# A new load order, fewer fillers, a shorter softmax and fewer copies at the start of a convolution and SwiGLU kernel

## The chip, the cores and the metric

The kernel runs on one core of one Trainium2 chip. The metric is the device time of one execution in microseconds (us); lower is better. It is about 1.8 us more than the span that the profile shows.

In this text TensorE is the matmul engine (PE in the profile, PEld for its weight loads), VectorE is DVE, ScalarE is ACT, GpSimd is POOL. L384 is a line of the kernel file. Each variant has its own file, so the same matmul has slightly different line numbers in different kernels.

## The reference, cut to what matters

```python
w = softmax(weight)                    # 8 heads x 7 taps
x_pad = zeros(6 rows) + x              # x: 8 x 4096 x 192, fp32
y = sum over k of w[h, k] * x_pad[s + k, head h]     # causal convolution of 7 taps
g = y @ w_gate                         # 192 -> 1536
out = (g * sigmoid(g) * (y @ w_val)) @ w_out         # 1536 -> 192, 32768 rows
```

## The kernel before

The 32768 rows are worked in 64 blocks of 512. In the steady state, each block takes 12 steps of gate and value matmuls (128 columns of the 1536 each), a SiLU on ScalarE, a product on VectorE, and the down projection, which trails behind. The convolution is itself a matmul with a band matrix made from the taps.

Blocks 0 to 3 have a special path (`early`), because nothing has been convolved when the kernel starts. The start has these parts.

The loads. All of them are issued from GpSimd, and they cast fp32 to fp16 on the way:

```python
    xe_load(0)                                  # x of block 0, three transfers
    for f0, f1 in ((0, 384), (384, 960), (960, Dff)):
        load_w(f0, f1)                          # gate and value weights, three transfers each
    xe_tile(1)
    xe_load(1)                                  # x of block 1, two transfers
    load_wo(0, 6)                               # down weights
    xe_tile(2)
    xe_load(2)
    load_wo(6, NCH)
    xe_tile(3)
    xe_load(3)
    # ... then the large x loads of the later blocks
```

The softmax of the taps, and its split into two fp16 parts:

```python
    seq(nc.vector.tensor_reduce(wmax, wraw, axis=AX.X, op=ALU.max))
    seq(nc.vector.tensor_scalar(wraw, wraw, scalar1=wmax, scalar2=None, op0=ALU.subtract))
    seq(nc.scalar.activation(wexp[:, 0:K], wraw, AF.Exp))
    # ... sum and reciprocal on VectorE
    seq(nc.vector.tensor_scalar(split[:, 0, 0:K], wexp[:, 0:K], scalar1=wsum, scalar2=None, op0=ALU.mult))
    # ... scalar_tensor_tensor writes split[:, 1], the rest
```

TensorE's own chain. Fillers are matmuls on zeros that only keep it busy:

```python
    keep_warm(11)         # 11 fillers, 128 x 512
    spread_taps()         # 16 tiny matmuls: taps to 128 partitions; VectorE then makes `spread`
    keep_warm(3)
    make_wide()           # 4 matmuls 128 x 512, then copies: the band matrix `wide`
    early(0, ...)         # convolution of block 0: 64 matmuls, then copies to `tme`
    eturn(0, ...)         # 15 transposes
    for n in range(n_steps):
        # ... after the gate and value matmuls of step 4: early(1), the convolution of block 1;
        #     step 7: first down projection; step 10: early(2)
```

The copies in `early`, four per block, two of them on each engine:

```python
        for hh in range(2):
            for r, (g0, g1) in enumerate(ER):       # 288 and 192 columns
                # ...
                seq((act, dve)[(hh + r) % 2](tme[e][...], o[...]))
        seq(dve(tme[e][:, :, SL * Q : 4 * Q], tme[e][:, :, 0:Q]))
```

## Time and profile before

| | |
|---|---|
| time, median of 3 runs | 796.1 us (795.15 to 796.2) |
| span of the profiled run | 794.0 us |
| TensorE busy | 784.4 us, 99% |
| TensorE waits for x of block 1 | until 16.44 us |

The first line below is from the profile's page (busy time, share of the span and number of instructions by engine). The second is the page's chain of work that ended last, by engine.

```profile
PE 784.4 (99%) x12023; PEld 494.3 (62%) x12023; DVE 584.7 (74%) x938; ACT 522.3 (66%) x910; POOL 67.4 (8%) x93
PE 97%; POOL 1%; DMA 1%; DVE 0%; ACT 0%; issue 0%; POOLq 0%
```

TensorE is the bound, and nearly all the idle time left is at the start. The next lines are TensorE's timeline there: start in us, duration in us, engine and line, operation, out<-in, count; in brackets the idle time before and what ended it.

```profile
1.20 4.21 PE L648 MATMUL warm<-fill 128*128 128x512 f16 x11 [1.20 <-DVE fill L91]
5.35 0.26 PE L290 MATMUL tapbank<-eye,split 8*32 8x8 f16 x16
5.54 0.82 PE L648 MATMUL warm<-fill 128*128 128x512 f16 x3
6.39 1.02 PE L330 MATMUL taps<-spread,shift 128*128 128x512 f16 x4
7.97 0.83 PE L384 MATMUL cv<-xe,wide 64*64 64x72 f16 x64 [0.56 <-ACT wide L342]
9.74 1.00 PE L443 MATMUL turn<-ident,tme 128*128 128x128 f16 x15 [0.95 <-DVE tme L403]
...
15.24 0.19 PE L384 MATMUL cv<-xe,wide 64*64 64x72 f16 x1 [0.65 <-DMA xe<-in_x_dram]
16.44 0.72 PE L384 MATMUL cv<-xe,wide 64*64 64x48 f16 x63 [1.01 <-DMA xe<-in_x_dram]
```

The first gate matmul is at 10.70 us, in the cut. The last two lines are the convolution of block 1, waiting for its x. The chain of waits in order of time (start, us, what) says why that x comes so late:

```profile
1.41 2.05 POOL xe L97 x3
3.46 4.70 POOL w L162 x8
...
8.88 0.65 POOL xe L97
9.53 6.87 DMA xe<-in_x_dram
```

GpSimd first issues x of block 0 and all nine weight transfers. Then x of block 1 is issued, and it needs almost 7 us behind them.

### The profile page before, as it was taken

The page shows a single profiled execution, that of the slowest core. Times are in us where ns is not written, and L with a number is a line of the kernel's source. Part 1 is how long each engine was busy: PE and PEld are TensorE (multiplying, and loading weights), DVE is VectorE, ACT ScalarE, POOL GpSimd, SP SyncE. Part 2 cuts the span into 40 slices and gives each one's busy share as a digit, 9 for nine tenths or more (in the row PEclk, how much of TensorE's full clock was granted, in tenths as well). Part 3 has the DMA queues.
Part 4 walks back from the last instruction along what each step waited for, and adds up shares of the span by engine and source line. Part 5 has one row for each costly group of instructions (what it writes and reads, how often), then busy time and mean ns, then how long its engine had stood idle before and what let it go on. Part 6 is the DMA issues. An engine that isn't in the chain of part 4 may idle for free.

```text
span 794.0 us, 28606 instructions
## 1 busy us (share of the span) xinstructions
PE 784.4 (99%) x12023; PEld 494.3 (62%) x12023; DVE 584.7 (74%) x938; ACT 522.3 (66%) x910; POOL 67.4 (8%) x93
## 2 busy tenths in 40 slices
PE   7999999999999999999999999999999999999997
PEld 3666666666666666666666666666666666666665
DVE  6777768777777777777777677777777777777775
ACT  5666666666666666766666666666666667666664
POOL 8111001010100101001010010100001010000000
PEclk9999999999999999999999999999999999999999
DMA  9999677785957778477795679857579884725311
GB/s 133 143 193 135 136 122 116 164 130 126 124 108 158 118 157 130 97 143 125 150 130 114 121 116 162 133 124 124 108 157 118 151 118 114 140 79 121 75 42 42
DMA packets 214961, 99.23 MB, mean 125 GB/s; under 512 B 148776, under 2 KB 213936, under 8 KB 213936
## 3 DMA queue, kind: packets, MB, share of 16 engines
q1 hardware_dynamic: 167424, 78.75, 48.7%
q0 software_dynamic: 47136, 18.45, 21.4%
q8 instruction: 94, 1.54, 0.8%
q14 instruction: 35, 0.29, 0.1%
q10 hardware_dynamic: 272, 0.20, 0.1%
HBM read 36.90 MB, written 41.16 MB: 98 GB/s over the span
## 4 chain that ended last, share of the span: by engine, by line
PE 97%; POOL 1%; DMA 1%; DVE 0%; ACT 0%; issue 0%; POOLq 0%
PE gate L550 61%; PE acc L576 32%; PE cv L474 2%; PE val L550 1%; DMA xe<-in_x_dram 1%; POOL w L162 1%; POOL xe L97 0%; PE acc L597 0%; PE cv L384 0%; PE turn L443 0%; DVE h L561 0%; ACT sig L559 0%; DVE o_sb L632 0%; DVE tm L491 0%; ACT o_sb L736 0%
## 5 line engine op out<-in xcount | busy, mean ns | idle before, releaser
L561 DVE TENSOR_TENSOR h<-sig,val 128x512 f16<-128x512 f16 x768 | 507.9, 688 | 196.0 <-PE val L550 190.7
L559 ACT ACTIVATE sig<-gate 128x512 f16<-128x512 f32 x768 | 458.7, 597 | 233.8 <-PE val L550 206.1
L550 PE MATMUL val<-xc,w 64*128 64x512 f16 x2304 | 539.1, 376 | 0.2 <-DVE tm L491 0.2
L550 PE MATMUL gate<-xc,w 64*128 64x512 f16 x2304 | 539.2, 376 | 0.0
L550 PEld LDWEIGHTS <-w 64*128 64x128 f16 x4608 | 221.1, 94 | 212.7 <-issue 1.6
L576 PE MATMUL acc<-wo,h 64*128 64x192 f16 x6096 | 298.9, 243 | 0.0
L576 PEld LDWEIGHTS <-h 64*128 64x128 f16 x6096 | 257.8, 94 | 66.0 <-issue 6.1
L97 POOL DMA_DIRECT2D x<-in_x_dram x40 | 31.6, 791 | 439.3 <-ACT sig L559 429.4
L491 ACT CAST tm<-cv 128x480 f16<-128x480 f32 x60 | 30.6, 562 | 22.1 <-PE cv L474 21.3
L491 DVE CAST tm<-cv 128x480 f16<-128x480 f32 x60 | 36.6, 652 | 2.5
L632 DVE COPY o_sb<-acc 128x384 f32<-128x384 f32 x63 | 34.7, 551 | 0.0
L502 POOL COPY tm<-tm 128x1280 f16<-128x1280 f16 x15 | 18.8, 1254 | 137.4 <-DVE tm L491 122.6
L631 ACT COPY o_sb<-acc 128x384 f32<-128x384 f32 x63 | 30.2, 479 | 0.0
L474 PE MATMUL cv<-x,band 64*32 64x240 f16 x960 | 18.2, 265 | 0.0
L474 PEld LDWEIGHTS <-band 64*32 64x32 f16 x960 | 10.1, 91 | 4.8 <-issue 4.6
L132 POOL MEMSET x<- 6x192 f16 x7 | 1.7, 248 | 59.7 <-PE cv L474 59.6
L648 PE MATMUL warm<-fill 128*128 128x512 f16 x14 | 5.0, 521 | 1.2 <-DVE fill L91 1.2
L403 ACT CAST tme<-cv 128x288 f16<-128x288 f32 (+1 forms) x8 | 2.9, 359 | 5.0 <-PE cv L384 3.6
L97 POOL DMA_DIRECT2D xe<-in_x_dram x9 | 6.0, 679 | 0.3 <-issue 0.3
L384 PE MATMUL cv<-xe,wide 64*64 64x48 f16 (+1 forms) x256 | 3.2, 192 | 2.2 <-DMA xe<-in_x_dram 1.7
L384 PEld LDWEIGHTS <-wide 64*64 64x64 f16 x256 | 2.7, 108 | 3.6 <-DMA xe<-in_x_dram 1.8
L403 DVE CAST tme<-cv 128x192 f16<-128x192 f32 (+1 forms) x8 | 2.9, 402 | 2.4 <-PE cv L384 2.4
(54 smaller groups left out, 40.7 us busy)
## 6 DMA issues: line engine op xcount, KB each, us to landing
out_dram<-o_sb SPq DMA_DIRECT2D x63, 384.0 KB
scr<-tm SPq DMA_DIRECT2D x105, 130.0 KB
x<-x SPq DMA_DIRECT2D x28, 480.0 KB
x<-in_x_dram POOLq DMA_DIRECT2D x24, 480.0 KB, 9.4
x<-in_x_dram POOLq DMA_DIRECT2D x7, 468.0 KB, 7.3
xc<-scr SPq DMA_TRANSPOSE x180
scr<-tm SPq DMA_DIRECT2D x15, 104.0 KB
wo<-in_moe_w_out_dram POOLq DMA_DIRECT2D x2, 288.0 KB, 6.9
```

Of the source, the lines that this page charges most:

```text
L97: nc.gpsimd.dma_start(out=t[p0 + i0 : p0 + i1, w0 - at : w1 - at, :], in_=bass.AP(tensor=x_flat.tensor, offset=(t0 + size * w0 - pad + i0) ...
L162: nc.gpsimd.dma_start(out=w16[Q * half : Q * half + Q, i0:i1, f0:f1], in_=src[Q * s0 : Q * (s0 + i1 - i0), f0:f1].rearrange("(s q) f -> q ...
L384: nc.tensor.matmul(o[Q * c : Q * c + Q, at : at + w], wide[Q * r : Q * r + Q, a, h, :], xe[e][Q * r : Q * r + Q, c : 2 * G : 2, h * grp : ...
L474: nc.tensor.matmul(banks[r][32 * c : 32 * c + 32, t * w : t * w + w], band[Q * r : Q * r + Q, h, :], x16[u][Q * r : Q * r + Q, NG * c : NG ...
L491: eng(tm[u][:, NG * r : NG * r + NG, 2 * grp * hp : 2 * grp * hp + 2 * grp].rearrange("p g (t e) -> p g t e", t=2), banks[r][:, 0 : 2 * w] ...
L502: seq(nc.gpsimd.tensor_copy(tm[u][:, :, SL * Q : 4 * Q], tm[u][:, :, 0:Q]))
L550: nc.tensor.matmul(o, w16[p0 : p0 + Q, k, ts(j, P)], xc[b][k][p0 : p0 + Q, 0:TB], start=(k == 0), stop=(k == SL - 1),)
L559: silu[n] = seq(nc.scalar.activation(sg, g, AF.Silu)).ins
L561: seq(nc.vector.tensor_tensor(hj, sg, v, op=ALU.mult))
L576: nc.tensor.matmul(acc[b][bank][:, s, :], hj[p0 : p0 + Q, ts(2 * bank + s, P)], wo16[p0 : p0 + Q, j, :], start=(not second and j == 0 and ...
L631: seq(nc.scalar.copy(o_sb[:, 0:2, :], acc[b][0]))
L632: seq(nc.vector.tensor_copy(o_sb[:, 2:4, :], acc[b][1]))
```

## The change

The intent is to shorten the start. x of block 1 goes ahead of the last weights, with fewer fillers in front of the taps, Exp taking the negated maximum as its bias (one VectorE operation less), and three larger copies instead of four.

```diff
-    for f0, f1 in ((0, 384), (384, 960), (960, Dff)):
-        load_w(f0, f1)
+    load_w(0, 384)
+    load_w(384, 1024)
     xe_tile(1)
     xe_load(1)
+    load_w(1024, Dff)
     load_wo(0, 6)
+    load_wo(6, NCH)
     xe_tile(2)
     xe_load(2)
-    load_wo(6, NCH)
...
-    seq(nc.vector.tensor_reduce(wmax, wraw, axis=AX.X, op=ALU.max))
-    seq(nc.vector.tensor_scalar(wraw, wraw, scalar1=wmax, scalar2=None, op0=ALU.subtract))
-    seq(nc.scalar.activation(wexp[:, 0:K], wraw, AF.Exp))
+    seq(nc.vector.tensor_reduce(wmax, wraw, axis=AX.X, op=ALU.max, negate=True))
+    seq(nc.scalar.activation(wexp[:, 0:K], wraw, AF.Exp, bias=wmax))
...
-        for hh in range(2):
-            for r, (g0, g1) in enumerate(ER):      # copies: ACT 288, DVE 192, DVE 288, ACT 192
+        for r, hh, n in ((0, 0, 4), (1, 0, H), (0, 1, 4)):   # ACT 288, DVE 384, ACT 288
...
-    keep_warm(11)
+    keep_warm(7)
     spread_taps()
-    keep_warm(3)
+    keep_warm(2)
     make_wide()
```

More of the change, by code (lines that the diff above doesn't have):

```diff
@@ L249 @@
     wmax = small("wmax", [H, 1])
-    seq(nc.vector.tensor_reduce(wmax, wraw, axis=AX.X, op=ALU.max))
-    seq(
-        nc.vector.tensor_scalar(
-            wraw, wraw, scalar1=wmax, scalar2=None, op0=ALU.subtract
-        )
-    )
-    seq(nc.scalar.activation(wexp[:, 0:K], wraw, AF.Exp))
+    seq(nc.vector.tensor_reduce(wmax, wraw, axis=AX.X, op=ALU.max, negate=True))
+    seq(nc.scalar.activation(wexp[:, 0:K], wraw, AF.Exp, bias=wmax))
     warmed = small("warmed", [P, 1], fp16)
@@ L397, in early @@
                         )
-        for hh in range(2):
-            for r, (g0, g1) in enumerate(ER):
-                w = 4 * (g1 - g0) * grp
-                o, at = ((bank[hh], 0), (bank[2], hh * w))[r]
-                seq(
-                    (act, dve)[(hh + r) % 2](
-                        tme[e][
-                            :, g0:g1, 4 * grp * hh : 4 * grp * (hh + 1)
-                        ].rearrange("p g (t e) -> p g t e", t=4),
-                        o[:, at : at + w].rearrange(
-                            "p (t g e) -> p g t e", t=4, g=g1 - g0
-                        ),
-                    )
+        for r, hh, n in ((0, 0, 4), (1, 0, H), (0, 1, 4)):
+            g0, g1 = ER[r]
+            o = bank[2] if r else bank[hh]
+            seq(
+                (act, dve)[r](
+                    tme[e][
+                        :, g0:g1, 4 * grp * hh : 4 * grp * hh + n * grp
+                    ].rearrange("p g (t e) -> p g t e", t=n),
+                    o[:, 0 : n * (g1 - g0) * grp].rearrange(
+                        "p (t g e) -> p g t e", t=n, g=g1 - g0
+                    ),
                 )
+            )
         seq(dve(tme[e][:, :, SL * Q : 4 * Q], tme[e][:, :, 0:Q]))
```

## The prediction

> **What bounds the kernel now.** TensorE. The page gives PE 784.4 us busy of a 794.0 us span (99%); the chain that ended last is 97% PE, and the clock row is 9 in every slice. From about 17 us on, the timeline shows PE without gaps. The change touches only the head (and the conv copies of blocks 0 to 3), so it can recover only head time.
>
> **The head, from the timeline.** Fillers start at 1.20 and every 0.43 us until about 4.6 (then half that); taps at 5.35, three fillers to 6.36, the wide matmuls 6.39 to 7.41, idle 0.56, conv of block 0 7.97 to 8.80, idle 0.95 (copies), transposes 9.74, first gate matmul 10.70. Then PE idles from about 14.6 to 16.44, but for one matmul, until x of block 1 lands. The chain of waits runs there: three x issues (1.41), nine weight issues to 8.9, then "DMA xe<-in_x_dram" 9.53 to 16.40. So anything saved before 14.6 alone is given back at that wait; the load order is the part that matters.
>
> **Each step.**
> 1. Fillers 11 to 7 and 3 to 2. Seven cold fillers end near 1.20 + 7 x 0.43 = 4.2. The taps need split, ready at 4.35 before. Removing the subtract (0.22 us) lets Exp start near 2.9 instead of 3.18; split should be ready near 4.1. Taps move from 5.35 to about 4.2, so the wide matmuls (gated by the 0.19 us tap copy and the first half of spread) start near 5.3. About -1.1 us. The Trainium skill, "TensorE: Matmul & The Clock Gate", Part 1, says the clock is at half rate until about 3.4 us of sustained activity; the 0.43 us spacing for 3.4 us agrees. With PE still busy, the switch should stay near 4.8.
> 2. Three copies: ACT 288 columns twice (0.40 us each), DVE 384 in one (about 0.5) instead of 192+288 (0.72) and a late ACT piece (9.27). Transposes start 0.3 us earlier. First gate matmul near 9.3.
> 3. Weights 384 to 1024: 11% more bytes, landing near 11.3 to 12.5 (11.2 to 12.3 before), while FFN step 3 would want them at 11.5: a new wait up to 0.6 us, hidden by the next one.
> 4. x of block 1: issued at 6.9 and 7.5 instead of 8.87 and 9.53. The queue drains in order at about 200 KB/us (of fp16 written), so it lands 432 - 48 = 384 KB earlier, about 1.9 to 2.6 us: near 14.2. PE is ready near 13.4, so this wait still binds, at 0.8 us instead of 1.8.
> 5. The last weights land near 16.2, needed after 19. The first six chunks of the down weights keep landing near 18.0 (same bytes ahead); they were needed at 20.09, now near 17.8: this caps the gain near 2.1 us.
>
> **Sum.** Raw gain about 2.2, capped near 2.1 us, all critical, 0.26%. Predicted 793.9 us, range 792.8 to 795.0. Faster by over 2%: 0.01; within 2%: 0.98; slower: 0.01.
>
> **What would show it.** Taps near 4.2; first gate matmul near 9.3; conv of block 1 starting near 14 in place of 16.44; the first down matmuls near 18 instead of 20.09, waiting on wo.
>
> **What would make it wrong.** The clock switching later, so the wide matmuls run at half rate; x of block 1 landing no earlier; the down-weight wait larger than 0.3 us; run-to-run spread (1 us among the three runs before) hiding the gain.

## The result, and the profile after

The changed kernel takes 793.86 us (median of 4 runs, 793.56 to 794.15), against 795.84 us for the kernel before (4 runs, 795.15 to 796.2). The ratio is 0.9976, 95% interval 0.9959 to 0.9993. The gain is about 2 us. It is within 2%, and the forecast of 793.9 us was nearly exact. All outputs are right.

The page's busy line, TensorE's timeline of the start, and the chain in order of time, all of the changed kernel:

```profile
PE 784.0 (99%) x12018; PEld 493.9 (62%) x12018; DVE 584.1 (74%) x933; ACT 522.2 (66%) x910; POOL 67.4 (9%) x93
```

```profile
1.20 3.17 PE L643 MATMUL warm<-fill 128*128 128x512 f16 x7 [1.20 <-DVE fill L91]
4.30 0.36 PE L286 MATMUL tapbank<-eye,split 8*32 8x8 f16 x16
4.59 1.03 PE L643 MATMUL warm<-fill 128*128 128x512 f16 x2
5.43 1.58 PE L326 MATMUL taps<-spread,shift 128*128 128x512 f16 x4
7.57 0.83 PE L380 MATMUL cv<-xe,wide 64*64 64x72 f16 x64 [0.56 <-ACT wide L338]
8.89 1.14 PE L438 MATMUL turn<-ident,tme 128*128 128x128 f16 x15 [0.50 <-ACT tme L398]
...
13.72 0.22 PE L380 MATMUL cv<-xe,wide 64*64 64x72 f16 x1
14.50 0.72 PE L380 MATMUL cv<-xe,wide 64*64 64x48 f16 x63 [0.56 <-DMA xe<-in_x_dram]
```

```profile
3.47 3.50 POOL w L162 x6
6.97 0.58 POOL xe L97
7.55 6.91 DMA xe<-in_x_dram
```

The conv of block 1, all but its first matmul, starts at 14.50 us instead of 16.44, which is 1.94 us earlier. From there both kernels run in step: from the sixth SiLU to the last of the 768, some thirty of them compared, the changed kernel is 2.0 us ahead (2.36 at one of them). So nothing is gained or lost after 18 us.

Two details do not fit the prediction. The taps start where it said (4.30 against about 4.2), but the four wide matmuls behind them take 1.58 us, where they took 1.02 before. The first gate matmul is therefore at 9.97 us, not at 9.3. And the removed subtract did not bring the taps' input forward at all. The experiments below look at both, and at the question of which part of the change is worth what.

### The profile page after: what moved, and what is told of

It is laid out like the page before. It is cut to its first block, busy times and chain, and to the rows that moved or that the text cites. A ratio compares the mean times of both kernels' runs of the same rounds, so it can differ in the third digit from the quotient of the medians.

```text
span 792.0 us, 28590 instructions
## 1 busy us (share of the span) xinstructions
PE 784.0 (99%) x12018; PEld 493.9 (62%) x12018; DVE 584.1 (74%) x933; ACT 522.2 (66%) x910; POOL 67.4 (9%) x93
## 4 chain that ended last, share of the span: by engine, by line
PE 97%; DMA 1%; POOL 1%; DVE 0%; ACT 0%; issue 0%; POOLq 0%
PE gate L545 61%; PE acc L571 32%; PE cv L469 2%; PE val L545 1%; DMA xe<-in_x_dram 1%; POOL w L162 0%; POOL xe L97 0%; PE acc L592 0%; PE cv L380 0%; PE turn L438 0%; DVE h L556 0%; ACT sig L554 0%; DVE o_sb L627 0%; DVE tm L486 0%; ACT o_sb L731 0%
## 5 line engine op out<-in xcount | busy, mean ns | idle before, releaser
L398 ACT CAST tme<-cv 128x288 f16<-128x288 f32 x8 | 2.9, 401 | 2.5 <-PE cv L380 2.5
L438 PE MATMUL turn<-ident,tme 128*128 128x128 f16 x45 | 3.3, 220 | 0.8 <-ACT tme L398 0.5
```

## The experiments

There were eleven runs, each on one chip. Five rounds were run per kernel, except where said (the run with one time is not in the table). Differences are the mean of the five times minus the mean of the nine times of the kernel before:

| kernel | mean us | before | difference | lowest to highest |
|---|---|---|---|---|
| new load order only | 794.56 | 795.58 | -1.02 | 793.97 to 795.30 |
| all but the load order | 796.45 | 795.58 | +0.87 | 795.94 to 796.74 |
| x still earlier | 793.58 | 795.58 | -2.00 | 792.83 to 794.40 |
| changed kernel again | 793.71 | 795.90 | -2.19 | 793.46 to 794.02 |
| all but the load order, again | 796.97 | 795.90 | +1.07 | 794.82 to 797.96 |
| load order and fillers only | 793.53 | 795.90 | -2.36 | 793.08 to 793.69 |
| x still earlier, six fillers | 793.57 | 795.90 | -2.32 | 793.04 to 794.67 |
| all but the load order, wait filled | 795.52 | 795.88 | -0.36 | 795.00 to 796.36 |
| loads by need | 792.67 | 795.88 | -3.21 | 792.23 to 793.26 |
| changed kernel, third time | 793.65 | 795.88 | -2.23 | 792.76 to 794.61 |

### The load order alone

```diff
 # the kernel before, with
-    for f0, f1 in ((0, 384), (384, 960), (960, Dff)):
-        load_w(f0, f1)
+    load_w(0, 384)
+    load_w(384, 1024)
     xe_load(1)
+    load_w(1024, Dff)
     load_wo(0, 6)
+    load_wo(6, NCH)
     xe_load(2)
-    load_wo(6, NCH)
```

> The kernel before with only the new load order (fillers 11 and 3, subtract kept, four copies). Theory A: the whole gain of 2.0 us is the earlier landing of x of block 1. Then x still lands near 14.5 us, the first gate matmul stays near 10.7, TensorE reaches the conv of block 1 near 14.6, so the wait there is about gone and the time is 0 to 0.3 us over that of the changed kernel, 1.6 to 2.0 us under the kernel before. Rival B: the earlier start of TensorE (0.73 us at the first gate matmul) is part of the gain; then this kernel gains only about 1.2 us.

It gained 1.02 us (ratio 0.9987, interval 0.9974 to 0.9999), half of the whole. That is close to rival B's 1.2 us. The interval, about 0.1 to 2.1 us, does not exclude theory A's 1.6 to 2.0; the run with fewer fillers below speaks against A too. The timeline of TensorE in this kernel:

```profile
6.01 0.27 PE L291 MATMUL tapbank<-eye,split 8*32 8x8 f16 x16
...
15.37 0.73 PE L385 MATMUL cv<-xe,wide 64*64 64x72 f16 x64
```

The conv of block 1 no longer waits for a transfer: there is no idle time before it, and its x had landed at 14.93 us. It starts at 15.37 because TensorE itself comes no sooner. With x out of the way, TensorE's own chain behind the long row of fillers is what bounds the start. Its taps start at 6.01 us instead of 5.35 with the very same fillers in front, because the clock switched later in this run. More on that below.

### All but the load order

```diff
 # the changed kernel, with the load order of before
```

> The changed kernel with the load order of before. Theory A: first gate matmul still near 10.0 us, but x of block 1 lands near 16.4 as before, the wait in front of its conv grows from 1.8 to about 2.5 us and the time is that of the kernel before, within 0.2 us. Rival B: it gains about 0.7 us. It also tells of the clock: if the late switch to full rate (near 6.5 us instead of 4.8) comes from fewer fillers, it is here too.

It did not gain, as theory A said. But it was 0.87 us slower than the kernel before, which neither theory had (ratio 1.0012, interval 0.9998 to 1.0026, so a difference of nothing is not quite excluded). The profiled run, the fastest of the five, had the span of the kernel before (794.1 us). The cause was therefore not visible, and the kernel was run once more.

> The changed kernel with the load order of before, once more. Its first profile gave the span of the kernel before (794.1 against 794.0), but its five times lay 0.9 us above it. If that was spread from run to run, the mean is now within 0.4 us of the kernel before; if the shorter head costs time with the old load order, it is again about 0.9 us above and the profile should show where: later x of block 1, or a wait behind it.

Again it was slower, by 1.07 us (ratio 1.0012, interval 0.9996 to 1.0028), with a wide spread (794.82 to 797.96 us), and this time the profiled run was the slowest of the five. Its timeline of TensorE:

```profile
15.57 0.21 PE L379 MATMUL cv<-xe,wide 64*64 64x72 f16 x1 [2.35 <-DMA xe<-in_x_dram]
16.11 1.17 PE L379 MATMUL cv<-xe,wide 64*64 64x48 f16 x63 [0.32 <-DMA xe<-in_x_dram]
17.21 0.61 PE L544 MATMUL gate<-xc,w 64*128 64x512 f16 x1
```

x landed at 16.06 us, no later than before (16.40). But the conv takes 1.17 us instead of 0.72, and a gate matmul 0.61 instead of 0.38. The granted clock explains the slower matmuls. The view below shows three stretches of this run: us, TensorE busy and matmuls, granted clock, DMA share, GB/s.

```profile
11.77:15.18 3.41, 1.45 (x12) 1.00 1.40 186
15.19:18.59 3.40, 2.70 (x72) 0.50 1.59 189
18.60:22.01 3.41, 3.41 (x27) 0.50 1.60 193
```

From 15.19 to 22.01 us, TensorE ran at half rate. In the stretch of 3.41 us before that, it had been busy for 1.45 us. The first profile of this kernel had a similar stretch and kept its clock, with slightly more work in it:

```profile
14.30:17.71 3.41, 1.72 (x73) 1.00 1.57 185
```

The Trainium skill, "TensorE: Matmul & The Clock Gate", Part 1, says that the clock is set by windows of 3.41 us: a busy window gives full rate, an idle one half rate. The traces agree on the length. The clock record of every trace shows a full-rate stretch that is a whole number of windows (785.065 us is 230 x 3.4133, 788.479 us is 231). So the shorter head did not merely fail to help with the old load order. It made the wait in front of block 1 longer (2.35 and 0.32 us, in place of 0.65 and 1.01 before), and in some runs the clock fell back behind that wait. That more than this one run was hit is an inference from the mean granted clocks of these five runs, 0.994 to 0.999, and from their spread. It need not be the whole loss: one of the five took 797.11 us at 0.998, a value that runs without such a stretch also show. Nor is the kernel before free of it, it seems: one of its nine runs took 797.87 us at 0.996. Without that run, its mean would be 795.65.

To test this, the wait was filled with ten more fillers.

```diff
 # all but the load order, with
             def work():
+                busy = apool.tile([P, TB], fp32, tag="acc0", name="busy")
+                for _ in range(10):
+                    seq(nc.tensor.matmul(busy, fill[:, 0:P], fill, start=True, stop=True,
+                                         skip_group_check=True))
                 early(1, (*acc_banks, gate_bank))
```

> The changed kernel with the load order of before, and ten further fillers between the fifth gate step and the conv of block 1, to keep TensorE busy while it waits for x. Theory H: the all-but-order kernel is slower than the kernel before because its longer wait (2.35 us in its second profile) lets the clock fall back to half rate for two windows (15.2 to 22.0 us there). Then, with the wait filled, no half-rate stretch comes between the first switch and the end in the profile, no run shows a granted clock of 0.997 or less, and the times are those of the kernel before within 0.4 us, with a spread under 1.5 us in place of 3. If the loss has another cause, the mean stays about 0.9 us over the kernel before.

It took 795.52 us on average, 0.36 us under the kernel before, with a spread of 1.36 us. No run showed a granted clock under 0.998, where the kernel without the extra fillers had gone down to 0.994. In its profile the fallback is gone; the same view, for the stretch that had been at half rate:

```profile
15.20:22.00 6.80, 6.63 (x137) 4.33 (x137) 3.51 (x7) 3.61 (x7) 5.75 (x10) 1.00 1.59 190
```

(This line lists all engines; the granted clock is the third number from the end.) All that theory H said came true, so it is well supported. Adding useless matmuls made this kernel 1.2 to 1.4 us faster, if differences from the kernel before are compared across calls.

### Load order and fillers, without the softmax and copy changes

```diff
 # the load-order-only kernel, with
-    keep_warm(11)
+    keep_warm(7)
     spread_taps()
-    keep_warm(3)
+    keep_warm(2)
```

> The kernel before with the new load order and fewer fillers only (subtract and four copies kept). Theory E: the load order moves the landing of x of block 1 to 14.1 to 14.9 us and thereby lays TensorE's own head bare, which in the order-only kernel reached that conv at 15.4; fewer fillers let the taps start at about 4.4, 1 to 1.6 us earlier. Then the conv of block 1 starts between 14.3 and 14.9 and the time is that of the changed kernel within 0.4 us: the subtract and the copies add little. Rival: the copies carry the rest, and this kernel is 0.8 us or more over the changed one.

It gained 2.36 us, where the changed kernel gained 2.19. So these two parts make the whole gain, and the shorter softmax and the three copies add nothing that shows. In its profile the conv of block 1 started at 13.55 us, sooner than in the first profile of the changed kernel and than the forecast of 14.3 to 14.9. The clock has a part in this: it switched at 4.77 us here and at 6.54 there (see below), and x landed at 13.41 us. A later wait then took some of it back:

```profile
13.55 0.73 PE L385 MATMUL cv<-xe,wide 64*64 64x72 f16 x64
...
18.10 1.16 PE L577 MATMUL acc<-wo,h 64*128 64x192 f16 x24 [0.71 <-ACT sig L560]
```

The timeline names ScalarE. The view of waits in the same stretch names the weight load in front of it, and the right cause:

```profile
PEld L577 <- DMA wo<-in_moe_w_out_dram: 1.2, 1, 1.2
PE acc L577 <- ACT sig L560: 0.7, 1, 0.7
```

The first down weights landed at 18.05 us. This is the cap that the prediction set for the down weights, seen here.

### Why removing the subtract did not help

The timelines of VectorE (the subtract, the multiplication, the rest) and GpSimd (the last issue for x of block 0, the first for the weights) in the kernel before, then that of VectorE in the changed kernel (GpSimd's line for the weights is the same there):

```profile
2.93 0.22 DVE L252 TENSOR_SCALAR wraw<-wraw,wmax 8x7 f32<-8x7 f32 x1
3.79 0.31 DVE L264 TENSOR_SCALAR split<-wexp,wsum 8x7 f16<-8x7 f32 x1
4.13 0.22 DVE L269 SCALAR_TENSOR_TENSOR split<-wexp,wsum,split 8x7 f16<-8x7 f32 x1
2.78 0.69 POOL L97 DMA_DIRECT2D xe<-in_x_dram  x1
3.41 0.70 POOL L162 DMA_DIRECT2D w<-in_moe_w_gate_dram  x1
```

```profile
3.64 0.47 DVE L260 TENSOR_SCALAR split<-wexp,wsum 8x7 f16<-8x7 f32 x1
4.14 0.22 DVE L265 SCALAR_TENSOR_TENSOR split<-wexp,wsum,split 8x7 f16<-8x7 f32 x1
```

The multiplication starts 0.15 us sooner and takes 0.16 us longer. In both kernels it ends at 4.10 to 4.11 us, within 0.02 us of when GpSimd has finished issuing the first weight transfer (3.41 + 0.70). The Trainium skill, "SBUF — State Buffer", section "Who interferes with whom", says that a `tensor_scalar` can run in a mode that needs a port pair shared with GpSimd, that whoever comes second is blocked until the other is done, and that `tensor_tensor` has no such mode (though with two inputs in SBUF it still contends with what GpSimd reads there). So the operation was replaced by a `tensor_tensor` (one round only):

```diff
-    nc.vector.tensor_scalar(split[:, 0, 0:K], wexp[:, 0:K], scalar1=wsum, scalar2=None, op0=ALU.mult)
+    nc.vector.tensor_tensor(split[:, 0, 0:K], wexp[:, 0:K], wsum.to_broadcast([H, K]), op=ALU.mult)
```

> The changed kernel with the tensor_scalar that writes the first half of split turned into a tensor_tensor with two SBUF inputs. Theory C: that tensor_scalar (0.47 us instead of 0.31, ending at 4.11 us in both kernels) is held until GpSimd has finished the issue of the first weight DMA (3.41 to 4.11), so the removed subtract bought nothing. Then the tensor_tensor takes under 0.2 us, split is ready near 4.0 instead of 4.36 and the taps start at 4.2, when the seventh filler is done. Rival D: something else, such as the order on VectorE, holds it; then it still ends near 4.1. The time stays that of the changed kernel within 0.3 us either way, since x of block 1 still lands near 14.5.

```profile
3.62 0.16 DVE L260 TENSOR_TENSOR split<-wexp,wsum 8x7 f16<-8x7 f32 x1
3.81 0.22 DVE L265 SCALAR_TENSOR_TENSOR split<-wexp,wsum,split 8x7 f16<-8x7 f32 x1
4.22 0.26 PE L286 MATMUL tapbank<-eye,split 8*32 8x8 f16 x16
```

It takes 0.16 us, split is ready at 4.03 us instead of 4.36, and the taps start when the seventh filler is done. Theory C holds: in all ten traces with the `tensor_scalar` it ends within 0.02 us of that issue, and in all three with the `tensor_tensor` it takes 0.16 us. The second operation now runs from 3.81 to 4.03 us in its usual 0.22 us, inside the stretch in which the multiplication had been held. That the port is what held it is the page's reason; the traces show only the times. They also show an exception: the removed subtract was a `tensor_scalar` too, started at 2.93 us during an issue of x (2.78 to 3.47), and took 0.22 us without being held to its end. The one time was 793.54 us, within the spread of the changed kernel. What the hold costs here is 0.3 us on VectorE, which the fillers hid but for 0.08 us.

### When the clock switches

The changed kernel was run twice more, with no edit.

> The changed kernel once more, beside the others of this call. Theory F: the switch of TensorE to full rate falls on the boundary of a free-running window of 3.413 us, so its time is a matter of the run and not of the fillers; in six profiles it came between 4.06 and 6.97 us. Then a second profile of the very same program may switch anywhere in about 4 to 7.4 us, and the full-rate stretch is again a whole multiple of 3.413 us. Rival G: with 7 and 2 fillers the switch is always late; then it comes at 6.5 us again, give or take 0.3. The time: 2.0 us under the kernel before, within 0.5.

The time was 2.19 us under the kernel before. The switch came at 6.42 us, which could not tell F from G.

> The changed kernel again, for a comparison on the same chip: 2.0 us under the kernel before, within 0.4. A third profile of the same program for the clock: the switch to full rate anywhere from 4.0 to 7.2 us after the start.

In the third profile of the same program, the switch came at 4.38 us. Rival G is refuted. The start of the full-rate stretch in the clock record of all thirteen traces:

```
kernel before            4.61        load order only          6.97
changed kernel           6.54, 6.42, 4.38
all but the load order   4.06, 4.95  wait filled              5.10
split as tensor_tensor   4.09        load order and fillers   4.77
x still earlier          6.85        six fillers              6.74
loads by need            4.94
```

TensorE is active from 1.20 us in all of them. The switch is a matter of the run, with 7 fillers and with 11 (4.61 and 6.97 us, in two kernels that differ in the load order). The traces fit theory F closely. Counted back from the switch in steps of 3.4133 us, the window that ends at the switch had TensorE busy for 2.86 us or more in every one of the thirteen traces, and the window before it for 2.35 us or less. So the switch came at the end of the first window that was busy for most of its length, and its time tells where the windows fell against the first filler at 1.20 us. A late switch makes the wide matmuls slow, and with 11 fillers it stretches the fillers as well. In the changed kernel the first SiLU starts 0.57 us later with the late switch of the first profile (6.54) than with the early one of the third (4.38). In that third profile the conv of block 1 starts at 13.15 us and the span is 790.9 us. This is probably one part of the spread of about 1 to 2 us that these kernels show. Another is the landing of x of block 1, which came at 14.46, 14.29 and 13.29 us in the three profiles. No run controls the window's phase, so what sets it stays open.

### x still earlier

```diff
 # the changed kernel, with
-    load_w(384, 1024)
+    load_w(384, 640)
     xe_load(1)
-    load_w(1024, Dff)
+    load_w(640, 1024)
     load_wo(0, 6)
+    load_w(1024, Dff)
     load_wo(6, NCH)
```

> The changed kernel with x of block 1 moved further ahead: weights 0 to 384, 384 to 640, x of block 1, weights 640 to 1024, first down weights, weights 1024 to the end, second down weights. Theory A: 288 KB less ahead of x, at 200 KB/us, so x lands near 13.0 instead of 14.5, but TensorE is only ready for it near 13.7; the conv of block 1 starts near 13.7 and the gain over the changed kernel is about 0.8 us, not 1.5. If the weights 640 to 1024 land after 14.4 part of that is given back just behind the conv. If x of block 1 were not what sets the time, nothing changes.

x landed at 12.21 us, 2.25 us sooner than in the first profile of the changed kernel. TensorE came to it at 13.86, so the conv was only 0.64 us sooner. The gain over the kernel before was 2.00 us, not told apart from the changed kernel's; the further 0.8 us that had been expected did not show. The switch was late here (6.85 us). Next, the split as `tensor_tensor` and six fillers were added to it.

> The kernel with x of block 1 ahead of the weights from 640, with the split as tensor_tensor and six fillers in place of seven. x of block 1 lands near 12.2 again, so TensorE's head alone sets the start of its conv. Taps start near 4.08, when split is done, instead of 4.22 to 4.30: conv of block 1 near 13.7 when the clock switches late, near 13.0 when it switches early. The time should be 0.3 to 0.9 us under the changed kernel of the same call. If the gain is under 0.2 us, the wait has moved elsewhere and the profile should name it.

The gain was 2.32 us, against 2.19 for the changed kernel: not told apart, and the profiled run was the slowest of the five. There the conv of block 1 started at 13.71 us, but the next one waited:

```profile
22.73 1.05 PE L381 MATMUL cv<-xe,wide 64*64 64x72 f16 x64 [0.80 <-DMA xe<-in_x_dram]
```

This is x of block 2, which landed at 22.69 and 23.02 us behind the second half of the down weights. The next wait in line had come up. The expected 0.3 to 0.9 us under the changed kernel was missed.

### Loads by need

```diff
 # x still earlier, six fillers, with
     load_w(1024, Dff)
-    load_wo(6, NCH)
     xe_load(2)
+    load_wo(6, 9)
+    load_wo(9, NCH)
```

> The loads ordered by when they are needed: weights to 640, x of block 1, weights 640 to 1024, first down weights, weights from 1024, x of block 2, down weights 6 to 9, 9 to 12, x of block 3; split as tensor_tensor, six fillers. The last try lost 1.3 us of its 2.7 in its profile where x of block 2 landed at 22.7 to 23.0, needed at 21.7. Here it should land near 20.5 to 21.5, with the down weights 6 to 9 near 22, so that the conv of block 2 does not wait. Then the time is about 0.5 us under the changed kernel of the same call (0.2 to 0.8). If it is not, another transfer has become late, and the profile should name it.

```profile
12.84 0.73 PE L382 MATMUL cv<-xe,wide 64*64 64x72 f16 x64
...
20.80 0.73 PE L382 MATMUL cv<-xe,wide 64*64 64x72 f16 x64
```

These are the convs of blocks 1 and 2. Neither has idle time before it: x of block 2 landed at 19.39 us. The time is 792.67 us on average: 3.21 us under the kernel before (ratio 0.9960, interval 0.9947 to 0.9972) and 0.98 us under the changed kernel. All five times are lower than twelve of the fourteen that the changed kernel gave. It is the fastest kernel, and 0.98 us is more than the 0.2 to 0.8 that had been expected. How much of it the later loads are worth is not settled. Against "x still earlier, six fillers" only they differ, but that kernel ran in another call, and its profile had the late clock switch (6.74 us, 4.94 here), which alone was expected to move the conv of block 1 from 13.0 to 13.7. What the profile does show of them is the landing of x of block 2, at 19.39 us in place of 23.02.

## Why the prediction was right or wrong

The time was right: 793.86 us measured, 793.9 predicted. A fit to 0.04 us is luck: the fourteen times of the changed kernel lie between 792.76 and 794.61 us, and x of block 1 landed between 13.29 and 14.46 us in its three profiles. The steps were right in part.

1. **"So anything saved before 14.6 alone is given back at that wait; the load order is the part that matters."** The first half was too kind. Without the load order the shorter head cost 0.9 to 1.1 us, at least in part because the longer wait let the clock fall to half rate in some runs. The second half is half the truth. The load order alone gained 1.02 us, because TensorE reached the conv of block 1 only at 15.37 us in its profile. Order and fillers together gained 2.36. The prediction took TensorE to be ready at 14.6, which holds only for an early clock switch.
2. **"With PE still busy, the switch should stay near 4.8."** Wrong. It came at 6.54 in the first profile of the changed kernel. It varies from run to run between 4.06 and 6.97 us, and in three profiles of the same program between 4.38 and 6.54. Hence the first gate matmul at 9.97 instead of 9.3. The list of what would make it wrong had named a later switch. It did not spoil the time because, in that profile, x of block 1 still came last.
3. **"split should be ready near 4.1."** Wrong: 4.36, as before, since the multiplication waited for GpSimd's issue. The taps at 4.30 were still near the predicted 4.2.
4. **Copies: "Transposes start 0.3 us earlier".** The mechanism was right, and the step was worth 0.45 us. From the start of the conv of block 0 to the transposes it took 1.77 us before (9.74 - 7.97) and 1.32 after (8.89 - 7.57). As long as x or TensorE's other steps decide, this shows nowhere in the time.
5. **x of block 1 "near 14.2", with a remaining wait of 0.8 us.** Right: 14.46, and 13.72 to 14.50. This was the step that carried the sum. The larger second weight slice landed at 11.35 to 12.58 us, as forecast ("11.3 to 12.5"), and its short wait stayed hidden behind the one for x.
6. **The cap by the down weights near 18.** In the first profile it did not bind: they landed at 17.61 and the matmul came at 18.15 without a wait. In the kernel with order and fillers only, it did bind (18.05).

## What to carry to other kernels

At the start of this kernel, several chains end at the same matmul: shortening one of them gained only up to the next, and with the old load order it even lost, with a longer wait behind which the clock fell back. So take the chains together, order the loads by the time at which each is needed, and read each wait after every step. And when a part of a change seems to be worth nothing, look for what it was hidden behind, here an issue on GpSimd and a row of fillers, before calling the idea wrong.

## What the Trainium skill lacked or had wrong

- "TensorE: Matmul & The Clock Gate", Part 1, puts the switch to full rate around 4 us into activity, with about 0.5 us of variation between runs. Here it came 2.9 to 5.8 us after the first matmul (4.06 to 6.97 us with activity from 1.20), and 2.2 us apart in profiles of the same program. So the 0.5 us is too small; the same Part also says that one kernel measured 6, 11 or 14 slow matmuls, which fits the wider spread. The window of 3.41 us that the page gives is confirmed.
- The same page says that the clock falls back after an idle window, and its table "Why this matters for your kernels" warns of gaps above about 3 us. Here a window in which TensorE was busy for 1.45 of 3.41 us was enough, with a longest wait of 2.35 us; one with 1.72 of 3.41 us was not. Half rate then lasted two windows, the first of which was busy for 2.70 of 3.40 us. The page gives no measure of how busy a window has to be. Over all thirteen traces, every full-rate window with 1.50 us or less of TensorE work was followed by half rate and none with 1.71 or more was; at half rate, 2.71 us or less never brought full rate and 2.86 or more always did.
- "SBUF — State Buffer", section "Who interferes with whom", agrees with the trace of the held multiplication. It gives no size for a small VectorE operation behind a transfer issue of GpSimd: here 0.31 to 0.47 us, to the end of the issue, where the `tensor_tensor` took 0.16. And it does not explain the subtract, a `tensor_scalar` of the same 8 x 7 elements that began 0.15 us into an issue of 0.69 us and was done in 0.22 us.
